# Retention attention followed by a snake MLP on one Trainium2 core: token layout of batch 4, a new hand-written order for blocks 0 to 2, and SBUF buffers from a table

## The chip, the cores and the metric

The kernel runs on one core of a Trainium2 chip. The metric is the time of one execution on the device in microseconds; the kernel before has a median of 307.27 us over 3 runs (306.55 to 307.67). The engines are TensorE (PE, with its weight loads PEld), VectorE (DVE), ScalarE (ACT), GpSimd (POOL) and SyncE (SP). SP only issues DMAs here. POOL and ACT issue a few as well.

## The reference

For 8 batches of 576 tokens and 8 heads of 64 the kernel computes a decayed causal attention, then a two-layer MLP with the "snake" function over all 4608 tokens. Inputs and output are float32; the kernel computes in float16 with float32 sums.

```python
scores = scale * np.matmul(q, k.transpose(0, 1, 3, 2))
Dmat = np.where(rel >= 0, gamma[:, None, None] ** rel[None, :, :], 0.0)   # rel = pos_i - pos_j
ret = scores * Dmat[None, :, :, :]
attn = np.matmul(ret, v)                       # -> x: 4608 tokens x 512
h = x @ w_in                                   # 512 -> 2048
s = np.sin(alpha * h)
out = (h + s * s / (alpha + 1e-09)) @ w_out    # 2048 -> 512
```

## The kernel before

**The work.** The first 512 tokens of each batch make one block of the MLP, block n for batch n; the last 64 tokens of all batches together make block 8. A block has 16 units. In unit `fc`, `project` (L516) makes 128 of the 2048 hidden values (4 matmuls of 512 columns), `sine` (L529, ACT), `square` (L537, ACT, DVE or POOL) and `product` (L546, DVE) make the snake of them. `gemm2` (L562) then multiplies 4 of the 16 hidden groups by one part of `w_out` (4 matmuls) for one of 4 token groups; 4 such calls make an output tile, which `finish` (L556) copies and stores. One block is thus 32 groups of 4 matmuls.

**The attention** of a batch needs q, k and v in two parts `p` of 256 tokens each. `load` (L110) fetches one part (512 KB) to one of six `raw` buffers; `cast` (L133) scales it by the decay and rounds it to float16, whole or by halves. `crossed` (L188) turns keys and queries with DMA transposes from SP; batches 0 and 1 use PE transposes instead (`turn` L196, `take` L209). Then come `scores` (L337), the mask on DVE (`masked` L355), `outer` (L270) with the running states (`take_sum` L307, `next_sum` L310, `more` L325 on POOL, `to_state` L316), `values` (L367), `add_states` (L400), and `keep` (L418), which writes the x of the next `project`.

**Two token layouts.** In batches below `HALVED` (L45, here 5) a partition holds two neighbouring tokens, so a load is one DMA with runs of 512 bytes. From `HALVED` on, keys and values lie in runs of 64 neighbouring tokens: L111 to L117 then issue four DMAs of 128 KB with runs of 256 bytes. In that layout half of the score block with `r = 1` is known to be zero: `scores` and `values` make 64 columns there where 128 were needed, and `masked` reads 768 elements of a partition and not 1024, with `mask_halved`, which POOL makes in unit 1 of block 3.

**The order.** The Tile framework keeps each engine's instructions in the order of the program text, and adds semaphore waits. For the constants, batches 0 to 3 and blocks 0 to 2 the order is written out by hand as some 480 lines (L637 to L1113). From block 3 on a loop (L1117) places attention pieces at given units. Every engine, and each DMA queue, runs strictly in that order: an instruction that waits holds up all behind it. Eight semaphores take turns at the DMAs of SP and ACT, so that each such DMA waits for the eighth before it.

**The start** (L637 to L700). SP loads k0, q0, v0, q1, k1, v1 of batch 0 (the digit is the part), then q1, q0, v0, k0, k1, v1 of batch 1. POOL issues `load_w_in` (L90) and `load_w_out` (L94), each group 1 MB read as float32 and written as 0.5 MB of float16: groups 0, 2, 1, 3 of `w_in`, then groups 0 to 3 of `w_out`. POOL also casts q1 of batch 1 (L680), which PE turns (L683) between the two `scores` of the second part. The first projection is `project(0, 2, "m1", 0)` (L700). `keep_busy` (L577) issues matmuls on zeros whose result nobody reads.

Of the kernel before, what the change touches and what calls it, by code (L numbers as in the profile page):

```python
# [13 lines left out]
MULT = mybir.AluOpType.mult  # L14


@with_exitstack
def kernel(
# [16 lines left out]
    nc = tc.nc  # L35
# [9 lines left out]
    HALVED = 5  # L45
# [59 lines left out]

    raw = {}
# [3 lines left out]
    def load(b, nm, p):  # L110
        if p < 2 and b >= HALVED and nm != "q":  # L111
            t_ = work.tile([P, H, 2 * D], F32, tag="raw", bufs=6, name=nm + "32")
# [6 lines left out]
        elif p < 2:  # L119
            t_ = work.tile([P, H, 2 * D], F32, tag="raw", bufs=6, name=nm + "32")  # L120
# [10 lines left out]
    nbuf = {"k": 4, "q": 3, "v": 4}  # L131

    def cast(b, nm, p, eng, ys=(0, 1)):  # L133
        t_ = raw[b, nm, p]
        if (b, nm, p) not in half:
            if p < 2:
                d_ = work.tile([P, 16 * D], F16, tag=nm + "16", bufs=nbuf[nm], name=nm + "16")
# [41 lines left out]
    def new_T(b, nm, p):  # L179
        if (b, nm, p) not in T:  # L180
            T[b, nm, p] = (
                work.tile([P, 8, P], F16, tag=nm + "T", bufs=4, name=nm + "T")
                if p < 2
                else work.tile([P, 4, P], F16, tag=nm + "Ts", bufs=B // 2, name=nm + "Ts")
            )
        return T[b, nm, p]
# [54 lines left out]
    class Attention:  # L241
# [11 lines left out]
        def tile(self, name, shape, dtype, bufs):  # L253
            if name not in self.tiles:
                self.tiles[name] = work.tile(shape, dtype, tag=name, bufs=bufs, name=name)
            return self.tiles[name]

        @property
        def x(self):
            xs[self.b] = self.tile("xT", [P, KT, 512], F16, 3)  # L260
            return xs[self.b]

        @property
        def kvs(self):
            return self.tile("kvs", [P, 4, 4, D], F32, 1)

        def state_of(self, c):
            return self.tile("s16", [P, 3, 4, D], F16, 2)[:, c] if c < 3 else sS[:, self.b]
# [56 lines left out]
        def more(self, c):  # L325

            s32 = work.tile([P, 4, D], F32, tag="s32", bufs=2, name="s32")
# [27 lines left out]
        def masked(self, p, y):  # L355
            sc = self.sc.pop((p, y))
            ret = work.tile([P, 2, 512], F16, tag="ret", bufs=4, name="ret")
# [171 lines left out]
    def sine(n, fc):  # L529
        hps = hps_of[n, fc][0]  # L530
        s_t = work.tile([P, 512], F16, tag="s", bufs=4, name="s_t")
# [5 lines left out]
    def square(n, fc, eng):  # L537
        s_t = hps_of[n, fc][1]
        ss_t = work.tile([P, 512], F16, tag="ss", bufs=4, name="ss_t")
# [56 lines left out]

    def make_constants():
# [30 lines left out]
    with tc.manual_schedule():  # L628
# [7 lines left out]

        load(0, "k", 0)  # L637
        load(0, "q", 0)
        cast(0, "q", 0, V, (1,))
        cast(0, "k", 0, V, (1,))  # L640
        cast(0, "k", 0, G_, (0,))
        load(0, "v", 0)
        cast(0, "v", 0, A_)
        keep_busy(16, "h0", 256)
        keep_busy(44, "op", 64)
        at[0].outer((0,), "h0", "h1")
        cast(0, "q", 0, V, (0,))
        turn(0, "k", 0, "op")
        turn(0, "q", 0, "h2")
        take(0, "k", 0, V, (0,))  # L650
        at[0].take_sum(0, V)
        take(0, "k", 0, A_, (1,))
        take(0, "q", 0, A_)
        load(0, "q", 1)
        cast(0, "q", 1, G_)
        load_w_in(0)
        load(0, "k", 1)
        cast(0, "k", 1, V)
        load_w_in(2)
        turn(0, "q", 1, "h0")  # L660
        at[0].scores(0, 1, "m0")
        turn(0, "k", 1, "h1")
        at[0].to_state(0, A_)
        take(0, "k", 1, A_)
        load(0, "v", 1)
        at[0].scores(0, 0, "m1")
        turn_alpha()
        take_alpha()
        keep_busy(10, "h2", 256)
        take(0, "q", 1, A_)  # L670
        load(1, "q", 1)
        at[0].take_sum(1, V)
        at[0].more(1)
        at[0].to_state(1, A_)
        cast(0, "v", 1, V)
        at[0].masked(0, 1)
        at[0].masked(0, 0)
        load_w_in(1)
        at[0].outer((1,), "h2", "h1")
        cast(1, "q", 1, G_)  # L680
        at[0].scores(1, 0, "m0")
        turn(1, "q", 1, "op")
        at[0].masked(1, 0)  # L683
        at[0].scores(1, 1, "m1")
        at[0].masked(1, 1)
        at[0].take_sum(2, A_)
        at[0].more(2)
        load_w_in(3)
        at[0].to_state(2, G_)
        load_w_out(0)  # L690
        at[0].values(0, False, "m0")
        at[0].values(0, True)
        at[0].add_states(0)
        at[0].values(1, False, "h0", "h2")
        load(1, "q", 0)
        take(1, "q", 1, A_)
        at[0].values(1, True)
        at[0].add_states(1)
        at[0].keep(0, V)
        project(0, 2, "m1", 0)  # L700
        at[0].keep(1, V, A_)
        project(0, 2, "m1", 1)
        sine(0, 2)
        project(0, 1, "op")
        keep_busy(2, "h0")
        square(0, 2, V)
        invert_alpha()
        product(0, 2)
        cast(1, "q", 0, G_)
        load(1, "v", 0)  # L710
        at[0].next_sum(3)
        sine(0, 1)
        square(0, 1, A_)
        project(0, 0, "h2")
        sine(0, 0)
        cast(1, "v", 0, A_)
        project(0, 8, "h0", 0)
        project(0, 3, "m0")
        sine(0, 3)
        project(0, 8, "h0", 1)  # L720
        product(0, 1)
        square(0, 0, V)
        product(0, 0)
        square(0, 3, G_)
        product(0, 3)
        project(0, 11, "m1")
        load_w_out(1)
        sine(0, 8)
        turn(1, "q", 0, "op")
        take(1, "q", 0, A_, (0,))  # L730
        sine(0, 11)
        take(1, "q", 0, V, (1,))
        project(0, 6, "h1")
        sine(0, 6)
        square(0, 6, V)
        at[0].to_state(3, G_)
        load_w_out(2)
        square(0, 11, A_)
        product(0, 6)
        product(0, 11)  # L740
        project(0, 7, "h2")
        sine(0, 7)
# [493 lines left out]
```

## Time and profile before

| what | value |
|---|---|
| median of 3 runs | 307.27 us (306.55 to 307.67) |
| profiled execution | 306.96 us, of which the span of its instructions is 305.2 us |
| PE busy | 293.5 us, 96% |
| DVE, ACT, POOL busy | 204.5, 182.7, 136.2 us |
| HBM read, written | 36.75 MB, 9.44 MB |

The profiled execution is 0.31 us under the median. "Span" runs from the first to the last instruction of the program, and 1.76 us lie around it. "Busy" of PE counts a matmul from its issue to its modelled end, so that a PE that is always busy can still be slowed by gaps in its pipeline. In a timeline a row is: start, duration of the group, engine, line, operation, tiles, shapes, number of instructions, and in brackets how long the engine stood idle before it and what ended the wait.

### The profile page before, as it was taken

How to read it: one execution, taken by the hardware profiler on the slowest of the kernel's cores; microseconds unless marked ns; L12 is line 12 of the kernel's file. 1: busy time of each engine (PE TensorE's matmuls, PEld its weight loads, DVE VectorE, ACT ScalarE, POOL GpSimd, SP SyncE). 2: the span in 40 equal slices, each digit the busy share in tenths (PEclk: the TensorE clock that was granted, in tenths of full speed). 3: DMA queues.
4: the chain of work that ended last, by engine and by line, in shares of the span. 5: the costliest groups of instructions: out<-in, count | busy, mean ns of one | idle time of the engine just before them, and what ended most of it. 6: DMA issues, size and time to landing. Idle time of an engine off the chain costs nothing.

```text
span 305.2 us, 7933 instructions
## 1 busy us (share of the span) xinstructions
PE 293.5 (96%) x3257; PEld 149.6 (49%) x3257; DVE 204.5 (67%) x296; ACT 182.7 (60%) x294; POOL 136.2 (45%) x155
## 2 busy tenths in 40 slices
PE   6879989999999999999999999999999999999995
PEld 5655556455444544454445444544454454444443
DVE  2768988899679796767665777566666746555600
ACT  1649935675365758665677567756764556555411
POOL 4794760498379488578039726653030000000000
PEclk9799999999999999999999999999999999999999
DMA  8999999997695978978689989866441111111132
GB/s 232 338 217 216 216 247 330 242 312 188 166 256 167 167 175 199 255 124 181 146 226 178 170 190 257 161 143 161 105 112 37 34 37 37 35 35 37 46 88 72
DMA packets 115508, 49.85 MB, mean 163 GB/s; under 512 B 69760, under 2 KB 110992, under 8 KB 115472
## 3 DMA queue, kind: packets, MB, share of 16 engines
q1 hardware_dynamic: 110912, 44.97, 62.8%
q0 software_dynamic: 4224, 4.19, 8.1%
q8 instruction: 25, 0.41, 0.6%
q10 hardware_dynamic: 336, 0.18, 0.3%
q14 instruction: 11, 0.09, 0.1%
HBM read 36.75 MB, written 9.44 MB: 151 GB/s over the span
## 4 chain that ended last, share of the span: by engine, by line
PE 82%; DMA 9%; POOL 3%; DVE 2%; ACT 1%; SPq 1%; issue 1%; DVEq 0%; ACTq 0%
PE ops L567 39%; PE hps L524 36%; DMA v<-in_v_dram 7%; PE sc L347 2%; PE o L389 2%; DMA q<-in_q_dram 2%; PE kv L283 1%; POOL q L169 1%; SPq L121 1%; POOL w_in L92 1%; PE o L411 1%; DVE ss_t L543 1%; DVE k L169 0%; DVE ret L359 0%; ACT v L102 0%
## 5 line engine op out<-in xcount | busy, mean ns | idle before, releaser
L567 PE MATMUL ops<-w_out,gT 128*128 128x512 f16 (+2 forms) x592 | 142.4, 373 | 0.9 <-DMA w_out<-in_moe_w_out_dram 0.4
L548 DVE SCALAR_TENSOR_TENSOR gT<-ss_t,inva,hps 128x512 f16<-128x512 f16 x144 | 106.2, 745 | 52.0 <-ACT ss_t L541 45.5
L532 ACT ACTIVATE s_t<-hps,alpha_t 128x512 f16<-128x512 f32 x144 | 97.3, 687 | 70.9 <-PE hps L524 68.1
L524 PE MATMUL hps<-xT,w_in 128*128 128x512 f16 (+1 forms) x544 | 126.5, 367 | 0.3
L524 PEld LDWEIGHTS <-w_in 128*128 128x128 f16 x608 | 58.6, 98 | 64.5 <-DVE xT L104 0.6
L567 PEld LDWEIGHTS <-gT 128*128 128x128 f16 x592 | 56.3, 98 | 65.0 <-issue 1.6
L543 DVE TENSOR_TENSOR ss_t<-s_t 128x512 f16<-128x512 f16 x72 | 43.6, 608 | 19.3 <-ACT s_t L532 18.7
L541 ACT ACTIVATE ss_t<-s_t 128x512 f16<-128x512 f16 x62 | 38.8, 632 | 0.9
L102 ACT COPY osb<-ops 128x512 f32<-128x512 f32 (+1 forms) x34 | 19.7, 582 | 22.0 <-PE ops L567 20.6
L169 POOL TENSOR_TENSOR k<-k,cn 128x1024 f16<-128x1024 f32 (+1 forms) x13 | 22.3, 1712 | 22.1 <-DMA k<-in_k_dram 17.9
L169 POOL TENSOR_TENSOR q<-q,cn 128x1024 f16<-128x1024 f32 (+1 forms) x16 | 27.2, 1710 | 10.9 <-DMA q<-in_q_dram 10.9
L359 DVE TENSOR_TENSOR ret<-sc,mask 128x1024 f16<-128x1024 f32 x20 | 23.9, 1219 | 4.2 <-PE sc L347 4.2
L329 POOL TENSOR_TENSOR kvs<-s,kvs 128x256 f32<-128x256 f32 x22 | 16.2, 734 | 4.0 <-ACT kvs L102 2.3
L543 POOL TENSOR_TENSOR ss_t<-s_t 128x512 f16<-128x512 f16 x10 | 10.8, 1084 | 14.6 <-ACT s_t L532 14.6
L102 ACT CAST xT<-o 128x1024 f16<-128x1024 f32 (+1 forms) x14 | 13.2, 957 | 6.1 <-PE o L411 5.9
L524 PE MATMUL hps<-xS,w_in 128*128 128x512 f16 x64 | 16.4, 379 | 0.0
L153 POOL TENSOR_TENSOR ks<-ks,cn 128x512 f16<-128x512 f32 x4 | 4.2, 1044 | 24.6 <-DMA vs<-in_v_dram 18.1
L104 POOL CAST v<-v 128x1024 f16<-128x1024 f32 (+1 forms) x10 | 10.0, 1007 | 11.1 <-DMA v<-in_v_dram 11.1
L328 POOL TENSOR_TENSOR s<-kvs,cn 128x256 f32<-128x256 f32 x22 | 14.3, 650 | 0.3
L321 POOL TENSOR_TENSOR s<-kvs,cn 128x256 f16<-128x256 f32 x19 | 12.2, 646 | 0.9 <-ACT kvs L102 0.4
L389 PE MATMUL o<-ret,v 64*64 64x128 f16 (+1 forms) x512 | 11.0, 214 | 0.9 <-DVE ret L359 0.4
L359 DVE TENSOR_TENSOR ret<-sc,mask_halved 128x768 f16<-128x768 f32 x12 | 11.4, 950 | 0.0
(62 smaller groups left out, 148.9 us busy)
## 6 DMA issues: line engine op xcount, KB each, us to landing
out_dram<-osb SPq DMA_DIRECT2D x70, 128.0 KB, 2.8
q<-in_q_dram SPq DMA_DIRECT2D x16, 512.0 KB, 5.4
k<-in_k_dram SPq DMA_DIRECT2D x10, 512.0 KB, 5.6
v<-in_v_dram SPq DMA_DIRECT2D x10, 512.0 KB, 6.4
k<-in_k_dram SPq DMA_DIRECT2D x24, 128.0 KB, 3.1
v<-in_v_dram SPq DMA_DIRECT2D x24, 128.0 KB, 3.3
w_in<-in_moe_w_in_dram POOLq DMA_DIRECT2D x4, 512.0 KB, 11.6
w_out<-in_moe_w_out_dram POOLq DMA_DIRECT2D x4, 512.0 KB, 11.5
```

Of the source, the lines that this page charges most:

```text
L102: eng.copy(d_, s_)
L169: eng.tensor_tensor(dst[:, a0:a1].rearrange("p a r t d -> p t (a r) d"), t_.rearrange("p (t a) x -> p t a x", t=2)[:, :, a0:a1].rearrange( ...
L328: nc.gpsimd.tensor_tensor(s32, self.kvs[:, c - 1], g1.unsqueeze(2).to_broadcast([P, 4, D]), MULT)
L329: nc.gpsimd.tensor_tensor(self.kvs[:, c], s32, self.kvs[:, c], ADD)
L359: nc.vector.tensor_tensor(ret.rearrange("p t (z x) -> p (t z) x", z=2)[:, :, 0:n], sc.rearrange("p t (z x) -> p (t z) x", z=2)[:, :, 0:n], ...
L389: made.append(matmul(o[t][halves(e), c : c + 128].rearrange("p (r i) -> p r i", r=2)[:, :, i0:64], v16[halves(g), 4 * t + 2 * x + e, r, :] ...
L524: matmul(hps_of[n, fc][0][:, cols], w_in16[:, a, fc * P : (fc + 1) * P], xs[n][:, a, cols], start=(a == 0 and part != 1), stop=(a == KT - ...
L532: nc.scalar.activation(s_t, hps, mybir.ActivationFunctionType.Sin, bias=0.0, scale=alpha_t[:, fc : fc + 1],)
L541: nc.scalar.activation(ss_t, s_t, mybir.ActivationFunctionType.Square)
L543: eng.tensor_tensor(ss_t, s_t, s_t, MULT)
L548: nc.vector.scalar_tensor_tensor(gT[n][:, fc, :], ss_t, inva[:, fc : fc + 1], hps, MULT, ADD)
L567: matmul(ops[n, c, cols.start][:, cols], gT[n][:, fk, c * P : (c + 1) * P], w_out16[:, fk, cols], start=(fk == 0), stop=(fk == FC - 1), sk ...
```

## The change

1. `HALVED` goes from 5 to 4: batch 4's keys and values have the second layout too.
2. The hand-written order of blocks 0 to 2 is replaced as a whole. The same pieces are computed; their order, the engines that do the casts, squares and states, the PSUM banks, and the matmuls on zeros are others. The loop from block 3 on is as before, except that its three PSUM tags start in the order h0, h2, h1, and that two of the loads of batch 5 come earlier in the list.
3. SBUF work buffers come from a table that names the slot for each use, where a pool handed them out in turn. Numbers of buffers per kind: six `raw`, four `k16`, three `q16`, four `v16`, four `kT`, four `qT`, two `s16`, three `xT`, four `ret`, `s` and `ss`, as before.
4. In block 7 three transfers of 16 KB from `w_out16` to a scratch tile are issued on SP. `wait_for_w_out(1)`, of the same kind, is used once in the new list.

```diff
-    HALVED = 5
+    HALVED = 4
+    places = {}
+    slot_of = {tag: iter(slots) for tag, slots in BUFFERS.items()}
+    def place(tag, shape, dtype):
+        name = tag + next(slot_of[tag])
+        if name not in places:
+            places[name] = work.tile(shape, dtype, tag=name, bufs=1, name=name)
+        return places[name]
...
-            t_ = work.tile([P, H, 2 * D], F32, tag="raw", bufs=6, name=nm + "32")
+            t_ = place("raw", [P, H, 2 * D], F32)
...
+    PAD = 3
+    def fill_up():
+        nc.sync.dma_start(gate, w_out16[:, 0, 0:64])
...
             if n == 7:
+                for i in range(PAD):
+                    at_unit(3 + i, fill_up)
```

The new list up to the first projection (the old one is L637 to L700 above):

```python
load(0, "k", 0); cast(0, "k", 0, V, (0,)); cast(0, "k", 0, V, (1,)); turn(0, "k", 0, "h0")
load(0, "q", 0); cast(0, "q", 0, V); keep_busy(3, "op"); turn_alpha(); turn(0, "q", 0, "h1")
take(0, "k", 0, A_, (1,)); take_alpha(); take(0, "k", 0, A_, (0,)); take(0, "q", 0, A_)
load(0, "q", 1); cast(0, "q", 1, G_, (0,)); cast(0, "q", 1, V, (1,)); load_w_in(2)
load(0, "k", 1); load(0, "v", 0); cast(0, "v", 0, G_); load(0, "v", 1); cast(0, "v", 1, G_, (1,))
load_w_in(0)
turn(0, "q", 1, "h2"); take(0, "q", 1, A_); at[0].scores(0, 0, "m0"); at[0].scores(0, 1, "m1")
cast(0, "k", 1, V)
load(1, "q", 1); cast(1, "q", 1, G_, (1,))
at[0].outer((0,), "h0", "h1"); cast(0, "v", 1, A_, (0,))
at[0].take_sum(0, V); at[0].to_state(0, V); at[0].take_sum(1, V); at[0].more(1)
load_w_in(1)
turn(0, "k", 1, "op"); take(0, "k", 1, A_); at[0].outer((1,), "h2", "h0")
keep_busy(13, "op", 128); at[0].scores(1, 0, "m0"); keep_busy(21, "h1", 128); at[0].scores(1, 1, "m1")
at[0].masked(0, 0); at[0].masked(0, 1); at[0].masked(1, 0)
cast(1, "q", 1, G_, (0,)); at[0].to_state(1, A_); invert_alpha(); at[0].masked(1, 1)
turn(1, "q", 1, "op"); take(1, "q", 1, A_, (1,)); take(1, "q", 1, A_, (0,))
at[0].take_sum(2, V); at[0].more(2); at[0].next_sum(3)
at[0].values(0, False, "m0"); at[0].values(0, True); at[0].to_state(2, G_)
load_w_in(3); load(1, "k", 0); cast(1, "k", 0, G_)
at[0].add_states(0); at[0].keep(0, A_); at[0].values(1, False, "h1", "h2"); at[0].values(1, True)
at[0].add_states(1); at[0].keep(1, A_, V); keep_busy(1, "h0")
project(0, 3, "m1", 0); project(0, 3, "m1", 1)
```

Further on in the new list: the loads of batch 1 follow in the order q1, k0, k1, q0, v0, v1; then `wait_for_w_out(1)` stands on SP ahead of nine loads of batches 2 and 3; the first `gemm2` is (0, 12) after 15 projections. Over the whole list casts on DVE, ACT and POOL go from 10, 4 and 16 to 3.5, 3.5 and 23 (a half counts 0.5), squares from 20, 18 and 10 to 13, 23 and 12, and `to_state` from 4, 2 and 14 to 3, 8 and 9.

852 lines of the change are left out of this document (432 added, 420 removed).

## The prediction

> **What bounds the kernel now.** First the page: the span, PE's busy time, and the chain that ended last.
>
> ```profile
> span 305.2 us, 7933 instructions
> PE 293.5 (96%) x3257; PEld 149.6 (49%) x3257; DVE 204.5 (67%) x296; ACT 182.7 (60%) x294; POOL 136.2 (45%) x155
> PE 82%; DMA 9%; POOL 3%; DVE 2%; ACT 1%; SPq 1%; issue 1%; DVEq 0%; ACTq 0%
> ```
>
> PE sets the time; no other engine is above 67%. So an edit counts only if it removes work from PE, or removes time in which PE waits. Second, the timeline of PE shows where it waits.
>
> ```profile
> 17.48 0.62 PE L202 MATMUL tr<-ident,q 128*128 128x128 f16 x8 [1.43 <-POOL q L169]
> 20.91 2.15 PE L524 MATMUL hps<-xT,w_in 128*128 128x256 f16 x12
> 22.90 0.59 PE L580 MATMUL idle<-zero 128*128 128x512 f16 x2
> 26.80 0.61 PE L202 MATMUL tr<-ident,q 128*128 128x128 f16 x8
> 27.24 6.34 PE L524 MATMUL hps<-xT,w_in 128*128 128x512 f16 x32
> ...
> 38.10 1.02 PE L567 MATMUL ops<-w_out,gT 128*128 128x512 f16 x4 [0.42 <-DMA w_out<-in_moe_w_out_dram]
> 40.23 1.89 PE L567 MATMUL ops<-w_out,gT 128*128 128x512 f16 x8 [0.25 <-ACT kvs L102]
> 44.67 0.45 PE L283 MATMUL kv<-v,k 64*64 64x64 f16 x32 [0.67 <-ACT v L102]
> 50.26 2.01 PE L524 MATMUL hps<-xT,w_in 128*128 128x256 f16 x13
> 101.69 6.22 PE L524 MATMUL hps<-xT,w_in 128*128 128x512 f16 x28
> ```
>
> Three stretches follow. The start ends at 20.91 with the first projection. Block 0 and the attention of batch 1 last until 50.26, where block 1 begins. The hand-written rest ends where `project(3, 0)` begins, the last of the seven groups in the 101.69 row, at 101.69 + 6 x 0.86 = 106.9. From there the chain of waits gives the steady pace:
>
> ```profile
> 112.22 0.86 PE hps L524 x4
> 113.66 0.97 PE ops L567 x4
> 143.27 0.86 PE hps L524 x4
> 144.60 0.97 PE ops L567 x4
> ```
>
> A group of four matmuls takes 0.86 us. Unit 3 of block 3 ends its scores at 113.66, that of block 4 at 144.60: 30.94 us for a block, of which 32 groups are 27.65 (32 x 0.864) and the attention of a batch the other 3.29. Against this pace the two listed stretches can be measured. From 20.91 to 50.26 PE does 16 projections and 9 `gemm2` (25 x 0.864 = 21.6), three turns of 0.45 (27.24 less 26.80) and one batch of attention (3.29): 26.2 of 29.35 us. **3.1 us are lost**, and the rows name them: two matmuls on zeros (0.43), waits for a `w_out` group, for ACT, for v of batch 1. From 50.26 to 106.9 there are 55 groups (47.5), two batches (6.6) and one more `outer` (about 0.3): 54.4 of 56.6. **2.2 us are lost**. So the new list can win at most 5.3 us behind the first projection; the rest depends on when that projection comes.
>
> **The change part by part.**
>
> *The start.* I walk the new list with durations of the old. When the inputs land is seen where engines start on them:
>
> ```profile
> 4.92 1.04 POOL L169 TENSOR_TENSOR k<-k,cn 128x512 f16<-128x512 f32 x1 [1.90 <-DMA k<-in_k_dram]
> 6.42 0.69 DVE L169 TENSOR_TENSOR q<-q,cn 128x512 f16<-128x512 f32 x1 [5.19 <-DMA q<-in_q_dram]
> 7.82 1.04 ACT L102 CAST v<-v 128x1024 f16<-128x1024 f32 x1 [4.55 <-DMA v<-in_v_dram]
> 9.36 1.90 POOL L169 TENSOR_TENSOR q<-q,cn 128x1024 f16<-128x1024 f32 x1 [3.40 <-DMA q<-in_q_dram]
> 11.21 1.68 POOL L92 DMA_DIRECT2D w_in<-in_moe_w_in_dram  x2
> 12.90 1.04 POOL L328 TENSOR_TENSOR s<-kvs,cn 128x256 f32<-128x256 f32 x1
> 15.51 1.92 POOL L169 TENSOR_TENSOR q<-q,cn 128x1024 f16<-128x1024 f32 x1
> 17.38 0.61 POOL L328 TENSOR_TENSOR s<-kvs,cn 128x256 f32<-128x256 f32 x1
> 18.07 0.73 POOL L329 TENSOR_TENSOR kvs<-s,kvs 128x256 f32<-128x256 f32 x1
> ```
>
> Loads land 1.5 us apart, whatever they hold; the first six of the new list (k0, q0, q1, k1, v0, v1) therefore at 4.9, 6.4, 7.8, 9.4, 10.9 and 12.4, an estimate for the last two. On POOL, half of q1 is cast from 7.8 to 8.9 and the first group of `w_in` issued at 8.9, which was 11.21 before. v0 is cast 10.9 to 11.9, half of v1 12.4 to 12.9, and `w_in` group 0, which the first projection reads, is issued at 12.9, 1.7 us later than before. Then POOL waits for the **seventh load, q1 of batch 1**, casts half of it (1.04), does `more(1)` (0.61 + 0.73), issues a `w_in` group (0.8), and casts the other half (about 1.0): 4.2 us from that landing until PE can turn q1 of batch 1. PE has all else done by 16.6 (the second `scores` of part 1 waits for a mask that ends at 15.8). All of `values` and `add_states` stand behind this turn.
>
> When does the seventh load land? Alone, 1.5 us after the sixth, at 13.9. But the stream of `w_in` slows SP's loads:
>
> ```profile
> 3.35 1.48 SPq L121 DMA_DIRECT2D q<-in_q_dram  x1
> 20.57 7.01 SPq L121 DMA_DIRECT2D v<-in_v_dram  x1
> ```
>
> ```profile
> 12.00:14.40 2.40, 2.28 (x50) 1.79 (x48) 2.40 (x4) 2.29 (x6) 2.31 (x4) 0.94 1.15 342
> 14.40:15.20 0.80, 0.80 (x8) 0.53 (x7) 0.80 (x2) 0.80 (x3) 0.80 (x2) 1.00 1.22 282
> 15.20:20.00 4.80, 2.85 (x129) 2.26 (x128) 3.26 (x4) 2.61 (x7) 4.68 (x6) 1.00 1.20 219
> ```
>
> An issue on SP takes 1.48 us while its queue has the DMA engines to itself and 7.01 beside the weights. In the windows (last column GB/s) the rate falls from 342 to 219 between 14.4 and 15.2, some 3.3 us after the first `w_in` issue. In the new list that point comes at 8.9 + 3.3 = 12.2, just as the seventh load begins to flow. Bounds: 13.9, if it slips through, and 12.4 + 7.2 = 19.6, if it is shared all along. I take 16.2: a part of it passes before the stream is at full rate, and the first `w_in` group can leave a gap before the next. [...]
>
> So the turn starts at 16.2 + 4.2 = 20.4. Behind it lie the turn and two half copies on ACT (1.65 in all) and a `keep` of 0.96 (a mean of the page, quoted under batch 4): first projection at about 23.0, **2.0 us later** than 20.91. Bounds: with 13.9 it would be 20.7, but then DVE decides: four masks of 1.2 from 13.4, then `take_sum(2)`, `more(2)` (1.34) and `to_state(2)` (0.6) put the last `add_states` at 20.9 and the projection at 21.5, which is also the earliest landing of `w_in` group 0 (12.9 + 8.5, the shortest of the four `w_in` transfers). With 19.6 it is 26.4. Range of this term: +0.6 to +5.5.
>
> The clock is part of it:
>
> ```profile
> 6.50:8.90 2.40, 0.00 (x0) 0.02 (x1) 1.81 (x3) 1.04 (x1) 0.00 (x0) 1.00 1.15 347
> 8.90:12.20 3.30, 3.20 (x56) 2.90 (x55) 1.64 (x3) 1.18 (x2) 2.84 (x3) 0.50 1.16 351
> ```
>
> After 2.4 us without a matmul the granted clock was 0.50 for 3.3 us. Before the first projection the old list has only the gap of 1.43 and keeps 1.00; the new one leaves PE idle from 16.6 to 20.4. I cost this at nothing in the forecast and price it as a rival. [...]
>
> *Block 0.* 3.1 us lost before. A later start gives the DMAs more time: of the waits at 38.10 and 44.67 (`w_out`, v of batch 1) and their pipeline refill little is left, and the two matmuls on zeros are gone. The weights are issued later too; the third `w_out` group and the `w_in` group of the fifth projection arrive about when PE wants them. I keep 1.1 of loss: **-2.0** (bounds -3.1 and +1).
>
> *Blocks 1 and 2.* The list takes 6.5 casts of 1.2 and 7 squares of 0.4 off DVE, some 10 us of its load, and gives ACT and POOL more.
>
> ```profile
> 50.20:107.00 56.80, 56.28 (x735) 28.78 (x733) 47.82 (x65) 34.59 (x56) 37.13 (x39) 1.00 0.93 220
> ```
>
> DVE had 47.8 of 56.8 us here, so the list is better balanced. But batches 2 and 3 load later, behind `wait_for_w_out(1)`, and their transposes stand behind nine loads. I take **-1.0** of the 2.2 lost (bounds -2.2 and +2).
>
> *Batch 4.* The gap for scores is 113.66 - 113.08 = 0.58 us with 128 columns and 144.60 - 144.13 = 0.47 with 64. Two such places save 0.22, `values` about 0.1: **-0.3**, on PE in a steady block, so in full (0.2 to 0.45). Four masks shrink on DVE, off the path. Four loads become 16 issues.
>
> ```profile
> L102 ACT CAST xT<-o 128x1024 f16<-128x1024 f32 (+1 forms) x14 | 13.2, 957 | 6.1 <-PE o L411 5.9
> ...
> out_dram<-osb SPq DMA_DIRECT2D x70, 128.0 KB, 2.8
> ...
> k<-in_k_dram SPq DMA_DIRECT2D x10, 512.0 KB, 5.6
> ...
> k<-in_k_dram SPq DMA_DIRECT2D x24, 128.0 KB, 3.1
> ```
>
> The first of these rows is the `keep` used above, the others give the time from issue to landing. Four DMAs of 128 KB in place of one of 512 KB are some 8 us more on SP's queue in blocks 1 and 2, ahead of the transposes of batch 3. Those are wanted at about 93 us and can leave SP by 80: nothing, and up to 2 us if that cover is gone.
>
> *The table and the three transfers.* The table adds no instruction; the slots decide which earlier reader a load or cast waits for, and that is in the terms above. The three transfers sit on SP in block 7, each waiting for the one before it, at most some 3 x 2.8 us, while only output tiles queue there and four buffers hold them: nothing, and the last rows of SP take the same semaphores as before.
>
> **Sum.** +2.0 - 2.0 - 1.0 - 0.3 = -1.3 on the profiled execution of 306.96 us: 305.7. That execution lies 0.31 under the median, so **306.0 us** for a median.
>
> **The rivals.**
>
> *Cold and late start (slower).* Decided by the seventh load: from a landing at about 17 on, PE idles more than 4 us. [...] For it: both fences above. Against: the matmuls on zeros ahead of 16 us, and that a gap of 1.43 did no harm.
>
> *The list loses nothing (faster).* 13.9 to 15 for the seventh load, start +1.0, block 0 -3.1 + 0.4, blocks 1 and 2 -1.7: 306.96 + 1.0 - 2.7 - 1.7 - 0.3 + 0.3 = 303.6. For it: DVE's relief, and that the losses were waits that an order can remove. Against: the same DMA bytes before 50 us.
>
> *New waits in blocks 1 and 2 (slower).* The transposes of batch 2 come after nine loads behind the `w_out` gate, and PE reaches the scores at about 63 us; each us that the data is late is a us of PE. With 3 us in place of -1.0: 310.0.
>
> *The layout does not pay.* If the later loads of batch 4 ate the 0.3, the time would be 306.3, inside the forecast.
>
> **How the numbers follow.** Forecast 0.45 (its own range 304.8 to 307.3), cold start 0.22, nothing lost 0.22, new waits 0.11. A measurement of this kernel can tell about 0.5%, 1.5 us, from no change: faster is below 305.7, slower above 308.8. Faster: 0.22 and 0.16 of the forecast, 0.38. Slower: 0.19 of the cold start and 0.08 of the new waits, 0.27. The rest, 0.35, is the same. Range 303.2 to 309.6: it reaches to the times of the first two rivals and leaves out the long ends of both.
>
> **What would show it.** The turn of q1 of batch 1 at 20.4, with PE's wait put down to POOL, and POOL's to a DMA of q; the first projection at 23.0; the granted clock 1.00 from there on. Block 1 starting near 50.3 although the first projection is 2 us later. Less DVE in the stretch to 107. Scores gaps of 0.47 in block 3. The forecast is wrong if the clock is 0.50 behind the first projection, if PE waits for transposes near 63, or if the seventh load lands by 14.

## The result and the profile after

The changed kernel takes 308.15 us (median of 20 runs, 306.86 to 309.97); the kernel before, on the same chips, 306.92 (20 runs, 306.05 to 307.91). The ratio is **1.0045, 95% interval 1.0035 to 1.0056: slower by 1.4 us**, where 306.0 was forecast. The time lies in the range, on the other side of no change. Here and below two executions that ran in a slower state (314.59 us with the inverse early, 311.8 with `w_in` ahead) are left out. The profiled execution took 309.24 us, 1.1 over the median. Its page, the lines for span, engines and chain of waits:

```profile
span 307.1 us, 7882 instructions
PE 290.3 (95%) x3215; PEld 145.7 (47%) x3215; DVE 192.1 (63%) x275; ACT 192.6 (63%) x325; POOL 144.0 (47%) x162
PE 81%; DVE 6%; DMA 4%; POOL 3%; SPq 2%; ACT 2%; issue 1%; DVEq 0%; ACTq 0%; POOLq 0%
```

PE has 3.2 us less to do (290.3 for 293.5) and still ends 1.9 later: it waits more. On the chain DVE has gone from 2% to 6% and DMA from 9% to 4%. PE's timeline of the changed kernel, the rows that answer to those of before:

```profile
15.33 1.35 PE L606 MATMUL idle<-zero 128*128 128x128 f16 x21
...
18.30 0.62 PE L228 MATMUL tr<-ident,q 128*128 128x128 f16 x8 [1.28 <-POOL q L195]
...
21.59 0.31 PE L437 MATMUL o<-qT,s 64*64 64x128 f16 x8 [0.52 <-POOL s L347]
...
22.16 3.64 PE L550 MATMUL hps<-xT,w_in 128*128 128x256 f16 x20
26.56 3.64 PE L550 MATMUL hps<-xT,w_in 128*128 128x512 f16 x20 [0.76 <-DMA w_in<-in_moe_w_in_dram]
...
32.11 3.62 PE L550 MATMUL hps<-xT,w_in 128*128 128x512 f16 x20 [1.47 <-DVE gT L574]
...
39.07 0.45 PE L309 MATMUL kv<-v,k 64*64 64x64 f16 x32 [0.37 <-DVE gT L574]
...
52.96 2.32 PE L550 MATMUL hps<-xT,w_in 128*128 128x512 f16 x10
...
87.93 1.02 PE L550 MATMUL hps<-xT,w_in 128*128 128x512 f16 x4 [1.05 <-DVE gT L574]
...
105.34 4.76 PE L550 MATMUL hps<-xT,w_in 128*128 128x256 f16 x24
109.94 1.03 PE L593 MATMUL ops<-w_out,gT 128*128 128x512 f16 x4
```

The turn of q1 of batch 1 starts at 18.30, the first projection at 22.16, block 1 at 52.96 and `project(3, 0)` at 109.94 - 0.86 = 109.08. In block 0 the rows name three waits: 0.76 for a `w_in` group, 1.47 and 0.37 for products of DVE; later 1.05 more.

Block 0's stretch now holds 10 `gemm2` and not 9, so its work is 26.2 + 0.86 = 27.1 us and that of blocks 1 and 2 is 54.4 - 0.86 = 53.5. With that, the two profiled executions compare so:

| piece | before | after | forecast | came |
|---|---|---|---|---|
| first projection | 20.91 | 22.16 | +2.0 | +1.25 |
| block 0, lost | 29.35 - 26.2 = 3.1 | 30.80 - 27.1 = 3.7 | -2.0 | +0.6 |
| blocks 1 and 2, lost | 56.6 - 54.4 = 2.2 | 56.1 - 53.5 = 2.6 | -1.0 | +0.4 |
| `project(3, 0)` to the span's end | 198.3 | 198.0 | -0.3 | -0.3 |
| around the span | 1.76 | 2.14 | 0 | +0.4 |
| sum | | | -1.3 | +2.3 |

So the question is why block 0 lost more and not less, though none of the waits that it had before is left in it. The "after" of this table is one execution: 1.1 of its +2.3 is its distance from the median, and a second profile of the same kernel ("changed kernel again" below) divides the loss otherwise: 4.1 in block 0, 1.4 in blocks 1 and 2.

### The profile page after: what moved, and what is told of

The parts are those of the page before. It is cut to its first block, busy times and chain, and to the rows that moved or that the text cites. A ratio compares the mean times of both kernels' runs of the same rounds, so it can differ in the third digit from the quotient of the medians.

```text
span 307.1 us, 7882 instructions
## 1 busy us (share of the span) xinstructions
PE 290.3 (95%) x3215; PEld 145.7 (47%) x3215; DVE 192.1 (63%) x275; ACT 192.6 (63%) x325; POOL 144.0 (47%) x162
## 4 chain that ended last, share of the span: by engine, by line
PE 81%; DVE 6%; DMA 4%; POOL 3%; SPq 2%; ACT 2%; issue 1%; DVEq 0%; ACTq 0%; POOLq 0%
PE ops L593 39%; PE hps L550 34%; PE o L415 2%; PE sc L373 2%; DVE gT L574 2%; DMA raw<-in_q_dram 2%; DMA raw<-in_v_dram 2%; SPq L149 1%; DVE ret L385 1%; PE kv L309 1%; DVE ss L569 1%; POOL q L195 1%; PE o L437 1%; ACT s L558 1%; POOL ss L569 1%
## 5 line engine op out<-in xcount | busy, mean ns | idle before, releaser
L574 DVE SCALAR_TENSOR_TENSOR gT<-ss,inva,hps 128x512 f16<-128x512 f16 x144 | 106.1, 746 | 66.2 <-ACT ss L567 54.7
L558 ACT ACTIVATE s<-hps,alpha_t 128x512 f16<-128x512 f32 x144 | 98.0, 686 | 68.2 <-PE hps L550 62.1
L569 DVE TENSOR_TENSOR ss<-s 128x512 f16<-128x512 f16 x65 | 37.1, 571 | 19.7 <-ACT s L558 19.1
L567 ACT ACTIVATE ss<-s 128x512 f16<-128x512 f16 x67 | 42.1, 631 | 1.3
L195 POOL TENSOR_TENSOR k<-raw,cn 128x1024 f16<-128x1024 f32 (+1 forms) x17 | 27.3, 1612 | 18.9 <-DMA raw<-in_k_dram 18.9
L195 POOL TENSOR_TENSOR q<-raw,cn 128x1024 f16<-128x1024 f32 (+1 forms) x18 | 28.6, 1601 | 9.2 <-DMA raw<-in_q_dram 9.2
L385 DVE TENSOR_TENSOR ret<-sc,mask 128x1024 f16<-128x1024 f32 x16 | 18.8, 1215 | 2.0 <-PE sc L373 2.0
L569 POOL TENSOR_TENSOR ss<-s 128x512 f16<-128x512 f16 x12 | 12.4, 1039 | 16.4 <-ACT s L558 15.2
L122 POOL CAST v<-raw 128x1024 f16<-128x1024 f32 (+1 forms) x14 | 13.4, 960 | 6.1 <-DMA raw<-in_v_dram 6.1
L179 POOL TENSOR_TENSOR ks<-ks,cn 128x512 f16<-128x512 f32 x4 | 4.2, 1042 | 23.4 <-DMA vs<-in_v_dram 11.5
L120 ACT COPY kvs<-kv 128x512 f32<-128x512 f32 (+2 forms) x13 | 7.3, 573 | 7.4 <-PE kv L309 6.3
```

Of the source, the lines that this page charges most:

```text
L120: eng.copy(d_, s_)
L122: eng.tensor_copy(d_, s_)
L195: eng.tensor_tensor(dst[:, a0:a1].rearrange("p a r t d -> p t (a r) d"), t_.rearrange("p (t a) x -> p t a x", t=2)[:, :, a0:a1].rearrange( ...
L385: nc.vector.tensor_tensor(ret.rearrange("p t (z x) -> p (t z) x", z=2)[:, :, 0:n], sc.rearrange("p t (z x) -> p (t z) x", z=2)[:, :, 0:n], ...
L558: nc.scalar.activation(s_t, hps, mybir.ActivationFunctionType.Sin, bias=0.0, scale=alpha_t[:, fc : fc + 1],)
L567: nc.scalar.activation(ss_t, s_t, mybir.ActivationFunctionType.Square)
```

## The experiments

**Theory 1:** waits that the new order itself makes (a DVE square held up by GpSimd, the inverse in the middle of the masks, `w_in` groups in an unsuitable order, q loads behind stores) cost the time, each its gap on PE. **Theory 2**, the rival: the start is bound by something broader, the half clock or the DMAs, and a wait that is mended reappears as another. Times are medians; the ratio is to the kernel before, run beside each. Span and positions are those of one profiled execution, which can lie up to 1.9 us from the median of its row.

| run | us | ratio (95%) | span | first projection | block 1 | `project(3, 0)` |
|---|---|---|---|---|---|---|
| changed kernel again | 308.9 | 1.0052 (1.0021 to 1.0084) | 307.2 | 23.0 | 54.3 | 109.2 |
| no pad | 308.98 | 1.0069 (1.0042 to 1.0097) | 307.8 | 22.4 | 54.4 | 109.3 |
| layout 5 | 309.35 | 1.0061 (1.0036 to 1.0087) | 305.5 | 23.8 | 52.3 | 107.3 |
| old list, layout 4 | 310.85 | 1.0116 (1.0088 to 1.0145) | 309.1 | 21.4 | 49.9 | 111.0 |
| inverse early | 309.01 | 1.0057 (1.0030 to 1.0084) | 305.1 | 22.8 | 52.1 | 107.2 |
| square on ACT | 308.8 | 1.0068 (1.0034 to 1.0102) | 305.1 | 22.4 | 51.3 | 107.0 |
| k1 in halves | 309.15 | 1.0087 (1.0058 to 1.0117) | 307.1 | 23.1 | 54.1 | 109.0 |
| `w_in` ahead | 308.75 | 1.0062 (1.0040 to 1.0085) | 306.0 | 23.4 | 51.9 | 108.0 |
| q loads early | 308.86 | 1.0075 (1.0061 to 1.0089) | 306.6 | 22.6 | 53.6 | 108.6 |
| `w_in` swapped | 308.62 | 1.0056 (1.0034 to 1.0077) | 305.0 | 23.3 | 51.7 | 106.9 |
| warm-up | 311.89 | 1.0133 (1.0099 to 1.0166) | 310.9 | 23.0 | 55.1 | 111.9 |
| four mends and warm-up (more matmuls) | 311.1 | 1.0130 (1.0103 to 1.0156) | 310.2 | 21.4 | 52.1 | 110.6 |
| shift only | 310.39 | 1.0126 (1.0110 to 1.0142) | 307.8 | 22.5 | 52.4 | 108.7 |
| warm-up, same count | 308.08 | 1.0067 (1.0033 to 1.0101) | 305.7 | 24.1 | 52.6 | 107.6 |
| four mends | 307.78 | 1.0039 (1.0023 to 1.0054) | 305.1 | 21.1 | 51.5 | 107.1 |
| four and warm-up, same count | 307.6 | 1.0027 (1.0008 to 1.0046) | 305.5 | 24.2 | 52.5 | 107.4 |
| four mends, reordered | 307.29 | 1.0016 (1.0003 to 1.0029) | 304.6 | 20.9 | 51.7 | 106.6 |

The changed kernel again had its first projection at 23.0 although its 21 matmuls on zeros took 1.35 us, as in the profile above, where 22.2 was expected for that case. From there to block 1 PE waits 0.41 us for `w_in` group 0, 2.08 at 32.98 and 0.41 at 40.38 for products of DVE, and not at 27; nor is there a gap at 88. So a gap that is missing in a run with an edit need not have been removed by the edit.

```profile
23.03 7.42 PE L550 MATMUL hps<-xT,w_in 128*128 128x256 f16 x40 [0.41 <-DMA w_in<-in_moe_w_in_dram]
...
32.98 3.62 PE L550 MATMUL hps<-xT,w_in 128*128 128x512 f16 x20 [2.08 <-DVE gT L574]
```

### The parts that the diff separates

No pad (`PAD = 0`, which leaves out the three transfers whose result nobody reads).

> The new kernel without the three transfers of block 7. If they cost nothing, the ratio to the kernel before stays 1.0045. If SP or the DMA semaphores at the end make them matter, the span after the last matmul (3.5 us in the kernel before) changes by more than 0.5 us.

The ratio does not differ from that of the changed kernel: no effect that can be measured.

Layout 5 (`HALVED = 5` in the new list, with `PAD = 7`), and the reverse, the old list with `HALVED = 4` and four such transfers in block 7:

> The new kernel with batch 4 in the old layout (HALVED 5, and seven transfers in block 7 in place of three, so that the last stores use the same semaphores). My theory: the layout saves 0.3 us of PE, so this is 0.3 us slower than the new kernel, ratio to before 1.005. Rival, the sixteen short transfers delay the loads of batch 3: this is faster than the new kernel by about 1 us, ratio 1.001, and PE's wait of 1.05 us at 87.9 is gone.

> The kernel before, with its own list and pools, and batch 4 alone in the new layout (four transfers in block 7 keep the semaphores of the last stores). My theory: 0.3 us faster than before, ratio 0.999. Rival, the short transfers cost: slower by 0.5 us or more, ratio 1.002 or above.

The layout alone, in the old list, costs 3.6 us. PE's timeline of that run:

```profile
101.73 0.19 PE L283 MATMUL kv<-v,k 64*64 64x64 f16 x1 [2.34 <-ACT v L102]
```

That is the `outer` of batch 4, whose loads of 128 KB come too late where the old list has them. The new list has no such gap. What the layout saves is looked for behind block 3: the stretch from `project(3, 0)` to PE's last matmul is 194.65 us with layout 5 and 194.49 in the changed kernel, and in the old list 194.79 before and 194.54 with layout 4. That fits 0.2 to 0.3, but the other profiles of the new list with layout 4 and no stop (below) lie between 194.3 and 194.8. In the times it is too small to show. The wait of 1.05 at 88 is not there with layout 5, as the rival has it; but it is not there in the changed kernel again either.

### The waits of block 0, one at a time

The wait of 1.47 at 32.11 goes back to this square on DVE, beside this cast on POOL (two timelines of the changed kernel, then the squares on DVE over the whole run, with least, median and most ns):

```profile
28.41 2.20 DVE L569 TENSOR_TENSOR ss<-s 128x512 f16<-128x512 f16 x1 [0.90 <-ACT s L558]
```

```profile
28.41 1.91 POOL L195 TENSOR_TENSOR k<-raw,cn 128x1024 f16<-128x1024 f32 x1
```

```profile
L569 DVE TENSOR_TENSOR ss<-s x65: 416/426/2203, 24.0 to 287.9; 128x512 f16<-128x512 f16 x65
```

A square that takes 0.43 us took 2.20, as long as the cast that began at the same moment and 0.3 beyond it. None of the 144 products of DVE, which read PSUM and SBUF, took over 0.75 us. My theory was that a square on DVE waits until a cast on POOL beside it ends; the 2.20 us here fit. Two runs were meant to test it: the square of piece 10 on ScalarE, and the cast of k1 cut in halves, which should shorten the wait.

```diff
-        square(0, 10, V)
+        square(0, 10, A_)
```

> The new kernel with the square of unit 10 of block 0 on ACT and not on DVE. My theory: on DVE it took 2.20 us and not 0.42, because it started beside POOL's 1.91 us cast of k1 and waited for its end; the product behind it was late, and PE waited 1.47 us at 32.1. On ACT the wait falls under 0.5 us and the total is 0.8 to 1.3 us lower, ratio 1.001. Rival, PE there waits for ACT, or the DMA sets the pace of block 0: PE's wait stays or moves to the next row, total unchanged.

```diff
-        cast(1, "k", 1, G_)
-        load_w_out(1)
+        cast(1, "k", 1, G_, (0,))
+        load_w_out(1)
+        cast(1, "k", 1, G_, (1,))
```

> The new kernel with POOL's cast of k1 of batch 1 in two halves of about 1.04 us, the third issue of w_out between them; the square stays on DVE. If DVE waits for the POOL instruction at hand to end, the square takes 1.0 to 1.4 us and not 2.20, PE's wait shrinks by 0.8 us, total 0.6 to 0.9 us lower. If DVE is slowed for as long as POOL is busy at all, the square takes 2 us or more as now, and the total stays.

The first run does not test it. In the list the squares of block 0 on DVE come in the order 3, 0, 7, 10, 13, 6, so the long one, the third of them, is that of **piece 7**, not of piece 10. In this run it is still on DVE, and it took 0.44 us (DVE, then POOL):

```profile
28.37 0.44 DVE L569 TENSOR_TENSOR ss<-s 128x512 f16<-128x512 f16 x1
```

```profile
28.48 0.80 POOL L113 DMA_DIRECT2D w_out<-in_moe_w_out_dram  x1
29.30 1.92 POOL L195 TENSOR_TENSOR k<-raw,cn 128x1024 f16<-128x1024 f32 x1
```

The gap at 32 is gone with this square short: it came 0.1 us ahead of POOL's DMA issue and was over before the cast. In the changed kernel again it came 0.2 us after the start of that issue, and took 2.82:

```profile
28.66 2.82 DVE L569 TENSOR_TENSOR ss<-s 128x512 f16<-128x512 f16 x1 [0.29 <-ACT s L558]
```

```profile
28.45 0.80 POOL L113 DMA_DIRECT2D w_out<-in_moe_w_out_dram  x1
29.28 1.91 POOL L195 TENSOR_TENSOR k<-raw,cn 128x1024 f16<-128x1024 f32 x1
```

There it began 0.6 us ahead of the cast and still ended 0.3 behind it; why is open. With the halves piece 7's square came early too (0.42), and the gap, now 1.89 at 35.4, goes back to the square of piece 10. DVE and POOL of that run:

```profile
31.09 3.44 DVE L569 TENSOR_TENSOR ss<-s 128x512 f16<-128x512 f16 x1
```

```profile
31.19 1.05 POOL L195 TENSOR_TENSOR k<-raw,cn 128x512 f16<-128x512 f32 x1
32.20 2.04 POOL L195 TENSOR_TENSOR q<-raw,cn 128x512 f16<-128x512 f32 x2
```

The square ended only at 34.53, some 0.3 after the third of three casts that follow each other. So cutting the cast did not help. It is not always so. With the q loads early, a square of DVE ended at 25.99, 0.3 behind a cast of POOL and 0.9 ahead of the POOL square that follows it (DVE, then POOL):

```profile
24.53 1.46 DVE L569 TENSOR_TENSOR ss<-s 128x512 f16<-128x512 f16 x1 [1.32 <-ACT s L558]
```

```profile
23.81 1.89 POOL L195 TENSOR_TENSOR k<-raw,cn 128x1024 f16<-128x1024 f32 x1 [0.99 <-DMA raw<-in_k_dram]
25.68 1.21 POOL L569 TENSOR_TENSOR ss<-s 128x512 f16<-128x512 f16 x1
```

A gap of over 1 us at 32 to 36 stands in the six profiles of the new list in which the square of piece 7 took 2.20 to 2.82 or, with the halves, that of piece 10 took 3.44. In the other eleven, where neither was over 1.7, the largest gap there that goes back to DVE is 0.93. Whether square and cast meet is a matter of some tenths of a us, and changes from run to run.

This also sorts the times. Three runs below have stops of another kind; of the other profiled executions of the new list, the five with such a long square took 308.65 to 309.83 us and the nine without it 306.73 to 308.08, where the kernel before has 306.9. So the long square goes with most of the loss. That it causes it is not shown: no run moves the square of piece 7 alone. The last run below does, among other things.

The other single edits: the inverse ahead of the masks, group 1 of `w_in` issued ahead of `more(1)`, groups 2 and 0 exchanged, and the two q loads of batches 4 and 3 ahead of the output stores.

> The new kernel with the inverse of alpha (two small DVE operations) computed behind the cast of k1 of batch 0, where DVE is idle, and no longer between the third and the fourth mask. My theory: in the start DVE's chain decides; the tensor_scalar of the inverse took 1.19 us beside a POOL cast where it took 0.17 before; without it the last add_states and the first projection come about 1.0 us earlier (21.1 and not 22.2), and the total is 0.8 to 1.1 us lower, ratio 1.001. Rival, the turn of q1 of batch 1 at 18.3 decides: the first projection stays within 0.3 us of 22.2 and the total too.

> The new kernel with the third group of w_in issued ahead of more(1) on POOL, 1.35 us earlier. My theory: PE's wait of 0.76 us for it at 26.6 is gone or below 0.2, the turn at 18.3 stays, total 0.5 to 0.8 us lower. Rival, the stream of weights runs without a gap, so that an earlier issue doesn't land earlier: the wait and the total stay.

> The new kernel with group 0 of w_in issued first (9.4 us) and group 2 second (13.0). My theory: group 0 lands at 22.0 to 22.8 in all runs of the new list, as late as the first projection; swapped it lands at about 18, and the first projection is set by DVE's masks and states alone, 21.8 to 22.2 at full clock; total 0.2 to 0.5 us lower than the new kernel. Rival, group 2 (fourth projection) then is late in its place and nothing is won.

> The new kernel with the loads of q1 of batches 4 and 3 put on SP behind the cast of k0 of batch 3, ahead of the last output tile of block 0. My theory: these loads stood on SP behind a store that waits for ACT (issued at 74.7); POOL waited 2.89 us for q1 of batch 3, its squares of block 2 came late, and PE waited 1.05 us at 87.9. Earlier by 5 us, POOL does not wait, PE's wait is gone, total 0.8 to 1.2 us lower. Rival, POOL has too much to do in this stretch: its squares stay late by more than 0.5 us, total lower by at most 0.4.

The last is for the gap at 87.93, which in the changed kernel goes from SP (eight stores, then the loads) to POOL (casts, then the squares), rows of SP and POOL:

```profile
64.93 9.74 SPq L586 DMA_DIRECT2D out_dram<-osb  x8
74.71 1.33 SPq L149 DMA_DIRECT2D raw<-in_q_dram  x2
```

```profile
81.82 2.90 POOL L195 TENSOR_TENSOR q<-raw,cn 128x1024 f16<-128x1024 f32 x2 [2.89 <-DMA raw<-in_q_dram]
...
86.05 2.04 POOL L569 TENSOR_TENSOR ss<-s 128x512 f16<-128x512 f16 x2
```

The chain is real: the gap stands only in this profile and in that with `w_in` ahead (1.01), the two in which POOL waited over 2.8 us for q. But with the q loads left where they are, POOL waited only 1.08 in the changed kernel again, PE had no such gap, and blocks 1 and 2 lost 1.4; with the loads early they lost 1.5. So this loss of 1 us belongs to some executions, and the edit can't be credited with its absence. Group 1 of `w_in`, issued earlier, still landed at 26.9, and its wait was gone only because PE came later: the rival of that run holds. With the inverse early PE waits 0.89 for `w_in` group 0 instead. **None of the edits moved the median**: 308.6 to 309.2, with 308.9 for the changed kernel as it is. Theory 1 as it stood, one gap one gain, falls for the inverse, group 1 of `w_in` and the q loads, whose intervals leave out the gains that were forecast. For the exchange of groups (0.2 to 0.5 us) they do not, and for the square of piece 7 there is no such run.

### The clock, and a place in the program

In some profiles of the new list the 21 matmuls on zeros ahead of the turn take nearly twice as long (2.39 us for 1.35). This is the run with `w_in` swapped, for the 15.33 row above (1.35):

```profile
16.82 2.39 PE L606 MATMUL idle<-zero 128*128 128x128 f16 x21
```

There the first projection comes at 23.3, in others with such a row at 23.4 and 23.8. The column of the granted clock reads 1.00 here, so the lower rate is read from the durations; but the trace's first record of the clock comes only at 19.05, and at 11.23 in the changed kernel's. To keep the clock up, 18 matmuls on zeros of 256 columns were put at the very start; a second run had all four mends besides.

> The new kernel with 18 matmuls of 256 columns on zeros ahead of everything, from 1.3 to about 5.2 us, where PE has nothing to do. My theory: the run-to-run spread of the new kernel (306.9 to 310) comes in part from a clock that is at half up to 10 to 19 us; with the warm-up the full clock is there by 9 us, the turn of q1 of batch 1 is at 18.3 in every run, the first projection at 22.2; median 0.4 to 0.8 us lower than the control. Rival, the later losses (DVE's square beside POOL's cast) depend on the start in the other direction, an early start meets the cast and waits: median unchanged or higher.

> The new kernel with the warm-up, the swapped w_in groups, the early inverse, the square of unit 10 on ACT and the early loads of q1 of batches 4 and 3. My theory: first projection 21.0 to 21.4, no wait of over 0.5 us at 27, 32 and 88, total 303.5 to 305.5, ratio 0.990 to 0.996, below both kernels. Rival, each wait removed only uncovers the next (weights, DVE): ratio above 1.000.

Both are slower by 2 to 3 us than the changed kernel, and not at the start. PE stands still in the middle, for nothing that the profile shows ("issue"). First the run with the warm-up, then that with the mends:

```profile
108.00 0.24 PE L437 MATMUL o<-qT,s 64*64 64x128 f16 x1 [1.55 <-issue]
...
199.00 0.30 PE L437 MATMUL o<-qT,s 64*64 64x128 f16 x5 [0.84 <-issue]
```

```profile
105.23 0.24 PE L437 MATMUL o<-qT,s 64*64 64x128 f16 x1 [1.72 <-issue]
...
198.37 0.30 PE L437 MATMUL o<-qT,s 64*64 64x128 f16 x5 [1.53 <-issue]
```

The times differ, but by count it is the same place: 1372 matmuls stand ahead of the first stop and 2392 ahead of the second, 1020 apart, in both (the forecasts below write 1371 and 2391). In the run with the mends the clock is 0.50 from 105.6 to 109.0, behind the first stop, which makes it dearer than its 1.72: the 24 matmuls behind it take 6.18 us, in the changed kernel 4.76. So either the place in PE's program does it, or the warm-up. One run has 18 matmuls of only 16 columns in their stead (same count, no warm-up), another the warm-up with 16 matmuls fewer later (21 of 128 columns became 5 of 512).

> The changed kernel with 18 zero matmuls of only 16 columns each ahead of everything: next to no work, but 18 more matmuls in TensorE's program, as in the run with the warm-up. Theory of the code position: TensorE stops again right before matmul 1371 (a matmul of o from qT and s, near 107 us) for about 1.5 us and before matmul 2391 (near 198 us) for about 1 us, so 310.8 us (309.5 to 312.5). Theory of the warm-up (the early matmuls themselves did the harm, by the clock or by starting things earlier): neither stop, 308.9 us (308.0 to 309.8).

> Warm-up of 16 zero matmuls of 256 columns at the very start, and the 21 zero matmuls of 128 columns ahead of the second scores become 5 of 512 (2560 columns for 2688), so that TensorE's program has the same number of matmuls as the changed kernel. Theory of the code position: no stop at 107 and 198 us, clock full from about 5 us; 308.0 us (306.8 to 309.2). If the half clock of the start is what costs the changed kernel its time, 307.3. Theory of the warm-up: 311 us again.

The run that only shifts the program:

```profile
104.76 0.24 PE L437 MATMUL o<-qT,s 64*64 64x128 f16 x1 [1.18 <-issue]
...
195.96 0.30 PE L437 MATMUL o<-qT,s 64*64 64x128 f16 x5 [1.05 <-issue]
```

The two stops are there again, behind the same two counts of matmuls, with 2.2 us in all, and 310.39 us; the warm-up without more matmuls has none and 308.08. With the four mends it is the same: stops with more matmuls, none at the same count (below). The place in the program is shown to be the cause. The traces also list the transfers of instructions, 16 KB each: before each of the six stops one begins 2.2 to 3.2 us ahead of PE's restart and ends 1.2 to 1.5 us ahead of it, while PE runs through some 150 short matmuls in 2 us. From these times I estimate that PE waits for instructions there. Why at these two places and at no other is not shown.

The warm-up itself did not secure the full clock. Windows of the run with the same count (the column behind POOL is the granted clock):

```profile
4.00:8.00 4.00, 2.25 (x16) 0.96 (x13) 2.21 (x3) 0.58 (x1) 0.00 (x0) 1.00 1.14 345
8.00:12.00 4.00, 3.10 (x49) 2.54 (x50) 2.22 (x3) 2.38 (x4) 2.66 (x3) 0.50 1.14 345
12.00:16.00 4.00, 2.99 (x90) 2.55 (x83) 2.55 (x5) 1.93 (x3) 3.33 (x5) 0.50 1.19 258
16.00:20.00 4.00, 4.00 (x43) 1.98 (x44) 2.47 (x4) 1.06 (x4) 3.36 (x5) 0.50 1.18 268
```

The clock fell at 8.0, after PE had been busy for 2.25 of the 4 us up to it, and came back only at 21.7; the first projection was at 24.1, and the time was as forecast all the same. With the four mends besides it was 0.50 from 7.9 to 21.5, in the run with the warm-up alone from 14.8 to 18.2, and in that with all five no half clock is on record before block 1. What decides is not shown.

### The mends together

> The four small mends that were run alone, together and without a warm-up: w_in group 0 fetched first, the inverse ahead of the masks, the square of the tenth piece on ScalarE, the two q loads of batches 4 and 3 issued ahead of the output stores. If the losses seen in the single profiles are what costs the time (0.6 of the first projection, 1.5 of the square, 1.0 of the q loads), 307.0 us (305.8 to 308.0), so 1.0 to 2 below the changed kernel. Rival, that each mend only moves the wait to the next thing: 308.6 (308.0 to 309.2), as with each alone.

> The four mends with the warm-up, at the same number of matmuls as the changed kernel: no stop at 105 and 198 us by the theory of the code position, and the first projection near 21.4 as in the run with all five; 306.0 us (305.0 to 307.5). By the theory of the warm-up 310.5 to 311.5; by the rival that mends only move the wait, 308 to 309.

Four mends (inverse, square of piece 10 on ScalarE, `w_in` swapped, q loads): 307.78, inside the range of the first forecast and under that of the rival. PE's timeline shows what is late next:

```profile
21.14 3.70 PE L550 MATMUL hps<-xT,w_in 128*128 128x256 f16 x20
26.55 3.64 PE L550 MATMUL hps<-xT,w_in 128*128 128x512 f16 x20 [1.72 <-DMA w_in<-in_moe_w_in_dram]
```

The first projection is as early as in the kernel before, and PE then waits for the third `w_in` group, which lands at the same 26.5 as in the changed kernel. The run with the warm-up added starts 3.0 us later (24.2) at the half clock, has no gap above 0.4 us, and is as fast (307.6, between its forecasts): what comes earlier only waits longer. The last run takes the need for that group two pieces later; the squares keep their places, so that piece 7's goes to ScalarE and piece 10's back to DVE.

```diff
-        project(0, 7, "m0")
+        project(0, 10, "m0")
...
-        project(0, 4, "m1")
+        project(0, 11, "m1")
...
-        project(0, 10, "op")
-        project(0, 11, "h1", 0)
+        project(0, 7, "op")
+        project(0, 4, "h1", 0)
```

> The four mends together, and pieces 10 and 11 of block 0 projected ahead of 7 and 4, so that the first six pieces need only the two groups of w_in that land first (22.1 to 22.2 us in these runs) and the third group (26.5 us) is needed two pieces of 0.86 us later. If the wait of 1.72 us before the third group was what was left of block 0's loss, block 1 starts near 49.8 (51.53 without the reorder) and the time is 306.2 us (305.3 to 307.3). If TensorE then only waits elsewhere in block 0 (w_out groups, the casts of batch 1 on GpSimd), block 1 starts at 51 to 52 and the time stays at 307.8 us (307.2 to 308.4).

Measured 307.29, ratio 1.0016, a time that both forecasts allow. The wait for `w_in` is gone, yet block 1 still starts at 51.7. PE, then POOL:

```profile
20.93 7.54 PE L550 MATMUL hps<-xT,w_in 128*128 128x256 f16 x40
...
34.25 0.62 PE L228 MATMUL tr<-ident,q 128*128 128x128 f16 x8 [1.05 <-POOL q L195]
```

```profile
29.47 1.89 POOL L195 TENSOR_TENSOR k<-raw,cn 128x1024 f16<-128x1024 f32 x1 [1.95 <-DMA raw<-in_k_dram]
```

Now POOL waits 1.95 for k1 of batch 1, casts it and q0 late, and PE waits for q0. So by the start of block 1 the second forecast holds: the wait moves, from `w_in` to the inputs of batch 1. In all, the ratio fell from 1.0045 to 1.0016, with intervals that do not overlap: the mends and the reorder together took back about two thirds of the loss. How much of that is due to piece 7's square, off DVE in this run alone, is not separated. No version beat the kernel before.

## Why the prediction was wrong, point by point

- **The step that failed is block 0, "-2.0".** It came out at +0.6. The waits at 38.10 and 44.67 and the matmuls on zeros did go, as forecast; what was wrong is "I keep 1.1 of loss". 1.1 is what is left beside named waits in the new kernel too (3.7 - 0.76 - 1.47 - 0.37), but 2.6 us of new waits came in: the third `w_in` group, of which I wrote that it arrives "about when PE wants" it, the square that took 2.20 us beside POOL's cast, and a product behind it. The term put at nothing is the casts that the list moves from DVE to POOL: in the five profiles of the new list with the long square of piece 7 a gap of 1.47 to 2.08 us stands behind it. Where no square was long and the first projection came at 23.2 to 24.2, block 0 lost 1.2 to 1.5, close to the 1.1; where it came at 20.9 and 21.1, 3.3 and 3.7.
- **"A later start gives the DMAs more time"** was half true. A start that is 3 us later loses little in block 0, an earlier one waits longer. In the eleven profiles of the new list without a square of over 2 us at 28 to 31, block 1 starts at 51.3 to 52.6, while the first projection ranges from 20.9 to 24.2. In the last run this is seen to be data: `w_in`, then k1 of batch 1. That it is data in all of them is argued from this.
- **The start, "+2.0", came at +1.25, by another cause.** The seventh load did not take until 16.2, and so one of the prediction's own signs of being wrong was there. POOL began its cast at 14.01 after waiting for it until then; the first packet of `w_in` moved at 12.99 and not at 12.2 (rows of POOL):

```profile
14.01 1.04 POOL L195 TENSOR_TENSOR q<-raw,cn 128x512 f16<-128x512 f32 x1 [0.23 <-DMA raw<-in_q_dram]
...
17.19 1.05 POOL L195 TENSOR_TENSOR q<-raw,cn 128x512 f16<-128x512 f32 x1
```

  The 4.2 us from there to the turn were right (14.0 to 18.3). So the case of my lower bound applied, in which DVE decides and `w_in` group 0 lands at 21.5; it came at 22.16 because of the inverse, 1.44 us of DVE amid the masks, that I had left out, and because that group landed at 22.1. With both mended (the four mends) it came at 21.14. In the changed kernel again it came at the forecast 23.0, with the turn at 18.7 and not 20.4: that agreement is luck.
- **Blocks 1 and 2, "-1.0", came at +0.4.** DVE was relieved as forecast. Windows of the changed kernel:

```profile
52.00:109.00 57.00, 55.75 (x726) 27.96 (x724) 37.60 (x48) 43.98 (x79) 41.46 (x42) 1.00 0.87 212
```

  37.6 us of DVE where 47.8 were. The new wait was not the transposes near 63 of the rival, it was the q loads behind the stores, which cost 1.05 in this execution. In the changed kernel again, without that wait, blocks 1 and 2 lost 1.4: the term is then -0.8, near the forecast.
- **Batch 4, "-0.3", fits** in size (198.3 to 198.0), though the runs that separate it (0.16 and 0.25) do not stand out of the scatter. The scores gap of 0.47 stands in the chain of waits in both blocks now, 30.82 us apart:

```profile
115.75 0.97 PE ops L593 x4
...
146.10 0.47 PE sc L373 x32
146.57 0.97 PE ops L593 x4
```

  The "up to 2 us if that cover is gone" is what the old list with this layout showed (2.34).
- **Table and transfers, "nothing"**: as forecast.
- **Around the span +0.4** was in no step. All 17 profiles of the new list have 2.03 to 2.14 us there, the two of the old list 1.76 and 1.89. The cause stays open.
- **The cold-start rival**, put at 308.9, was near the measured time but had the clock in the wrong place: the lower rate comes ahead of the turn, and costs an estimated 1 to 1.5 us of start in some executions (2.39 less 1.35 us; 23.3 to 23.8 less 22.16). No run shows the 2 us that it put on a half clock behind the turn: where the clock was 0.57 from 20 to 24 us (shift only), the first projection came at 22.5, and block 1 at 52.4, not behind the 52.96 of the changed kernel. That PE's late first matmul (5.69) brings it is argued, not shown. The profiles speak against it as the cause of the lost time: the three with such a row and no long square took 307.08 to 308.08.

## What to carry to other kernels

Price what a new order makes late, not only the waits that it removes: follow each group of weights and each load from issue to landing against the new time of need. Where a start is bound by data, an edit that takes out one gap of a profile can lengthen the next (here six edits alone gave 308.6 to 309.2 us, where the unchanged kernel had 308.9), so judge it by the interval of the times, and mend several together. Profile the unchanged kernel twice before you explain a gap, and count through the order of the program which instruction a row is before you edit one. When a program grows by a few instructions, look for a stop at a fixed count of instructions (here two of them, 2.2 us, with 18 more matmuls) before putting the change of time down to the edit.

## What the runs showed of the hardware

- **A DVE square took up to 3.44 us beside POOL instructions.** Its median is 0.43 us. The 3.44 were beside three casts that follow each other, and it ended 0.3 us behind the third. Another, with a cast and a square of POOL beside it, took 1.46 and ended 0.3 behind the cast.
- **A place in the program cost 0.8 to 1.7 us.** With 18 more matmuls PE stopped behind 1372 and 2392 matmuls in three kernels, whatever the 18 did.
- **A warm-up did not secure the clock.** With one until 4.8 us, and PE busy for 2.25 of the 4 us up to 8.0, the clock was 0.50 from 8.0 to 21.7. Without one, the 21 matmuls on zeros took 1.35 us in one profile and 2.39 in another. What decides is not shown.
